# Small row vectors on another DMA queue, their transpose earlier, and one weight block in one load: a fused state-space and MLP kernel on one core

## The chip, the cores and the metric

The kernel runs on one core of a Trainium2 chip. The metric is the device time of one execution in microseconds (us). The profile is a recording of one such execution by the hardware profiler. Its span is a little shorter than the device time, because it begins with the first recorded instruction and ends with the last.

The engines are named as in the profile: PE is TensorE (matmuls and transposes), DVE is VectorE, ACT is ScalarE, POOL is GpSimd, and SP is SyncE, which here only issues transfers. SP, ACT and POOL each have a queue from which they can start DMA transfers.

## The reference, cut to what matters

A sequence `x` of 2048 rows and 640 columns goes through two branches, and a gate mixes them:

```python
g = sigmoid((x * gate_w).sum(-1, keepdims=True))
# A: a diagonal complex state-space layer
dt = exp(log_dt)
Lam_bar = exp(dt * Lam)                       # Lam = Lambda_re + 1j * Lambda_im, 640 values
B_bar = ((Lam_bar - 1.0) / Lam)[:, None] * B
Bu = x @ B_bar.T
for t in range(L): h = Lam_bar * h + Bu[t]    # the scan over the sequence
a = 2.0 * real(hseq @ C.T) + x * Dskip
# B: an MLP
b = gelu(x @ w1 + b1) @ w2 + b2               # w1: 640 x 1728, w2: 1728 x 640
return g * a + (1 - g) * b
```

Four small vectors are of interest here: `Lambda_re`, `Lambda_im` and `log_dt` with 640 values each, and `b1` with 1728.

## The kernel before: the parts that the change touches

The kernel is written as operations with an engine, an assumed duration, the tiles that they read and write, and a priority. A small list scheduler in the kernel's own source fixes each engine's order of instructions when the program is built: of the operations that are ready in its simulated time it takes the one with the lowest priority number. Only the order comes from it; on the chip the engines wait for each other by semaphores.

The transfers of the beginning, all on SP's queue, bring in `x` (first 512 rows) and `w1` in blocks of 128 rows:

```python
NW = 8; FW = NW * 128                         # the first pass covers 1024 of the 1728 columns of w1
WSPLIT = {1: 6, 3: 6}

def w1load(k, eng, prio):
    edges = [0] + ([WSPLIT[k] * 128] if k in WSPLIT else []) + [FW]
    for i, (f0, f1) in enumerate(zip(edges, edges[1:])):
        load(f"w1_{k}{i}", eng, f"l_w1{k}{i}", W1sb[:, k, f0:f1], B_w1[k * 128:(k + 1) * 128, f0:f1],
             [("w1", k, i)], prio=prio + 0.1 * i, lat=2.6)

load("xna", "sp", ...)                        # x, first two column blocks, rows as they are
w1load(0, "sp", 1); w1load(1, "sp", 1.3)
xtrans(0, range(KN, KN + 1), 1.6, 0.8)        # x, third column block, transposed by the DMA
w1load(2, "sp", 2)
xtrans(0, range(3, 4), 3, 0.8)
w1load(3, "sp", 4)
xtrans(0, range(4, 5), 4.5, 0.8)
w1load(4, "sp", 5)
# ... the rest of w1 (w1_r0, w1_r1), then B, transposed by the DMA in 512 and 128 rows
```

The small vectors are needed as columns, one value for each partition. They are loaded as rows of 128 values into one tile `rows`, which PE transposes in one instruction into bank 7 of PSUM; DVE copies the result to `cols`:

```python
ROWS = {"lre": (0, A_Lambda_re), "lim": (KP, A_Lambda_im), "ldt": (2 * KP, A_log_dt), "b1a": (3 * KP, B_b1[0:nmain])}
op("rz", "pool", 0.2, (), list(ROWS) + ["b1b"], f_rz, prio=-90)     # rows <- 0
for i, (nm, (r0, src)) in enumerate(ROWS.items()):
    src = src.rearrange("(k p) -> k p", p=128)
    load(nm, "pool", "l_" + nm, rows[r0:r0 + src.shape[0], :], src, [nm], prio=-50 + i, dur=1.0)
load("b1b", "act", "l_b1b", rows[RT:RT + 1, :]..., B_b1[nmain:F]..., ["b1b"], prio=-101, dur=1.2)

psC = PS[7][:, :].bitcast(BF16)[:, 0:128]
def f_cols():                                                       # line 446 of the profile
    return inc("pe", nc.tensor.transpose(psC, rows[:, :], ident[:, :]))
op("cols", "pe", 0.3, list(ROWS) + ["b1b", "ident"], [("bank", 7)], f_cols, prio=20.5)
def f_cols1():                                                      # line 451
    return inc("dve", nc.vector.tensor_copy(out=cols[:, :], in_=psC[:, 0:RT + 1]))
op("cols1", "dve", 0.2, [("bank", 7)], ["lcol", "b1col"], f_cols1, prio=-1000)
```

From `cols` a chain of short operations goes over ACT and DVE: `dt = exp(log_dt)`, `acol = dt * Lambda_re`, `thcol = dt * Lambda_im`, the angles reduced to one turn, their sines on ACT (lines 456 to 490). ACT loads a function table for exp, one for sin and one for GELU. Only then, in ACT's order, comes the first GELU, which has `b1` from `cols` as its bias.

PE's first pass over `w1` goes block by block of 128 rows (`k`), with one PSUM bank for each group of 128 columns (`jf`), so that it can begin with the first block and keeps all eight banks open until the last block. The first four matmuls are halves of 256 columns:

```python
def m1_first():
    seq = [(k, jf) for k in range(KD) for jf in range(NW)]          # KD = 5, NW = 8
    seq.remove((0, NW - 1)); seq.insert(seq.index((1, NW - 1)), (0, NW - 1))   # bank 7 begins late
    steps = [(0, 0, 0), (0, 1, 0), (0, 0, 1), (0, 1, 1)] + [(k, jf, None) for k, jf in seq if k or jf > 1]
    for k, jf, h in steps: ...                                      # one matmul each, line 640
    for jf in range(NW):                                            # GELU of each bank, line 649
        op(f"ge_0_{jf}", "act", ..., [("bank", jf), "b1col"], [("gl", 0, jf)], f_ge, prio=10)
```

After these 42 matmuls the second pass (line 662) takes the remaining columns of `w1`, beginning with bank 0, which the first GELU must have read by then. After it come the products with B (line 705), the scan on DVE, and so on for four quarters of the sequence; none of that is touched by the change.

Of the kernel before, what the change touches and what calls it, by code (L numbers as in the profile page):

```python
# [147 lines left out]
class Prog:  # L148
# [8 lines left out]
    def op(self, name, eng, dur, reads, writes, fn, prio=None, lat=0.0, after=()):  # L157
        deps = {}
        for k in reads:
            for w in self.last_w.get(k, ()):  # L160
                deps[w.idx] = w
        for k in writes:
            for w in self.last_w.get(k, ()):
                deps[w.idx] = w
            for r in self.last_r.get(k, ()):
                deps[r.idx] = r
        for a in after:
            deps[a.idx] = a
        deps = list(deps.values())
        E = self.E  # L170

        def run(eg, deps=deps, eng=eng, fn=fn):
            E.wait(eng, *[d.done for d in deps if not (eng == "pe" and d.eng == "pe")])
            return fn()

        it = self.sch.add(name, eng, dur, deps, run, prio=prio, lat=lat)
        for k in writes:
            self.last_w[k] = [it]
            self.last_r[k] = []
        for k in reads:  # L180
            self.last_r.setdefault(k, []).append(it)
        return it


def bass_gated_mix__ssm_conv_s5__dense_activation_gelu__prompt_kernel(
# [40 lines left out]
    with ExitStack() as es:  # L226

        def SB(name, shape, dt):
            return es.enter_context(nc.sbuf_tensor(name, list(shape), dt))
# [12 lines left out]
        rows = SB("rows", [128, 128], BF16)  # L242
        cols = SB("cols", [128, 3 * KP + NF], FP32)
# [10 lines left out]
        ident = SB("ident", [128, 128], BF16)  # L254
# [53 lines left out]
        op = pr.op  # L308
# [4 lines left out]
        def dma_inc(eng, ins, sem):  # L313
            SEM(sem)
            E.count.setdefault(sem, 0)
            ins.then_inc(sems[sem], 16)
            E.count[sem] += 16
            return (sem, E.count[sem])
# [11 lines left out]
        def load(name, eng, sem, dst, src, writes, prio, dur=0.5, lat=2.5, reads=(), after=()):  # L330
            def fn():
                with nc.allow_non_contiguous_dma(reason="columns of small vectors"):
                    return dma_inc(eng, engines[eng].dma_start(dst, src), sem)
            return op(name, eng, dur, reads, writes, fn, prio=prio, lat=lat, after=after)
# [19 lines left out]
            load_T(f"xT{q}_{ks[0]}", f"l_xT{q}_{ks[0]}", [(xT[q][:, ks[0]:ks[-1] + 1, :], x2[q * 512:(q + 1) * 512, ks[0] * 128:(ks[-1] + 1) * 128])],  # L354
                   [("xT", q, k) for k in ks], prio, dur)

        WSPLIT = {1: 6, 3: 6}

        def w1load(k, eng, prio):
            edges = [0] + ([WSPLIT[k] * 128] if k in WSPLIT else []) + [FW]  # L360
            for i, (f0, f1) in enumerate(zip(edges, edges[1:])):
                load(f"w1_{k}{i}", eng, f"l_w1{k}{i}", W1sb[:, k, f0:f1], B_w1[k * 128:(k + 1) * 128, f0:f1], [("w1", k, i)], prio=prio + 0.1 * i, lat=2.6)

        def w1tok(k, jf):
            return ("w1", k, int(jf >= WSPLIT.get(k, NW)))

# [15 lines left out]
        ROWS = {"lre": (0, A_Lambda_re), "lim": (KP, A_Lambda_im), "ldt": (2 * KP, A_log_dt), "b1a": (3 * KP, B_b1[0:nmain])}  # L382
# [5 lines left out]
        op("rz", "pool", 0.2, (), list(ROWS) + ["b1b"], f_rz, prio=-90)  # L388
        for i, (nm, (r0, src)) in enumerate(ROWS.items()):
            src = src.rearrange("(k p) -> k p", p=128)  # L390
            load(nm, "pool", "l_" + nm, rows[r0:r0 + src.shape[0], :], src, [nm], prio=-50 + i, dur=1.0)
        load("b1b", "act", "l_b1b", rows[RT:RT + 1, :].rearrange("o (a p) -> o a p", a=2),
             B_b1[nmain:F].rearrange("(o p) -> o p", o=1).unsqueeze(1).broadcast_to([1, 2, FL]), ["b1b"], prio=-101, dur=1.2)

# [25 lines left out]
        for i, (k, c0, c1) in enumerate(((0, 0, 2), (0, 2, 4), (1, 0, 2), (1, 2, 4))):  # L420
            bank = (7, 6, 5, 4)[i]
# [23 lines left out]
        def f_cols():  # L445
            return inc("pe", nc.tensor.transpose(psC, rows[:, :], ident[:, :]))

        op("cols", "pe", 0.3, list(ROWS) + ["b1b", "ident"], [("bank", 7)], f_cols, prio=20.5)

        def f_cols1():  # L450
            return inc("dve", nc.vector.tensor_copy(out=cols[:, :], in_=psC[:, 0:RT + 1]))
# [642 lines left out]
```

## Time and profile before

| | before |
|---|---|
| device time, median of 3 runs | 214.33 us (214.19 to 214.42) |
| span of the profile | 212.5 us |
| PE busy | 209.4 us, 99% |
| DVE busy | 190.0 us, 89% |
| ACT busy | 102.9 us, 48% |
| POOL busy | 6.4 us, 3% |
| granted PE clock | 1.0 |
| first matmul of the first pass (L640) | 4.58 us |
| row transpose on PE (L446) | 9.46 us |
| first GELU (L649) | 13.92 us |
| second pass (L662) begins | 14.75 us |

An L and a number is a line of the kernel's source. In a line of the chain the first number is the start in us, the second the duration, and `x21` the number of instructions merged in that piece. In a line of the timeline the form is the same, with the tile that is written and the tiles that are read (`out<-in`), and in square brackets the idle time before it with what ended it. `ACTq` and `SPq` are the queues' instructions that issue a transfer; the time shown is that of issuing it and not that of the transfer. What a transfer takes is given as the time from its issue to its landing.

### The profile page before, as it was taken

How to read it: one execution, taken by the hardware profiler on the slowest of the kernel's cores; microseconds unless marked ns; L12 is line 12 of the kernel's file. 1: busy time of each engine (PE TensorE's matmuls, PEld its weight loads, DVE VectorE, ACT ScalarE, POOL GpSimd, SP SyncE). 2: the span in 40 equal slices, each digit the busy share in tenths (PEclk: the TensorE clock that was granted, in tenths of full speed). 3: DMA queues.
4: the chain of work that ended last, by engine and by line, in shares of the span. 5: the costliest groups of instructions: out<-in, count | busy, mean ns of one | idle time of the engine just before them, and what ended most of it. 6: DMA issues, size and time to landing. Idle time of an engine off the chain costs nothing.

```text
span 212.5 us, 2752 instructions
## 1 busy us (share of the span) xinstructions
PE 209.4 (99%) x1102; PEld 104.8 (49%) x1102; DVE 190.0 (89%) x240; ACT 102.9 (48%) x177; POOL 6.4 (3%) x16
## 2 busy tenths in 40 slices
PE   8999999999999999999999999999999999999996
PEld 4444444444464444444464444444446444567775
DVE  2199999999999999999999999999999999497954
ACT  2099556667960253556671063455660027623330
POOL 5000000030000000000010000000010000000000
DMA  5999999999800020046375000002854000005711
GB/s 169 192 281 179 152 140 220 347 244 190 188 7 3 0 49 0 0 28 155 67 58 114 3 0 0 0 2 71 111 117 123 0 3 0 0 0 102 170 39 62
DMA packets 48879, 19.07 MB, mean 90 GB/s; under 512 B 41572, under 2 KB 47844, under 8 KB 48868
## 3 DMA queue, kind: packets, MB, share of 16 engines
q1 hardware_dynamic: 47136, 17.59, 40.2%
q0 software_dynamic: 1728, 1.32, 4.9%
q8 instruction: 8, 0.13, 0.3%
q14 instruction: 3, 0.02, 0.1%
q10 hardware_dynamic: 4, 0.00, 0.0%
HBM read 8.41 MB, written 2.63 MB: 52 GB/s over the span
## 4 chain that ended last, share of the span: by engine, by line
PE 96%; ACT 1%; DVE 1%; issue 0%
PE ps L662 22%; PE ps L705 20%; PE ps L929 20%; PE ps L978 15%; PE ps L792 7%; PE ps L841 5%; PE ps L640 2%; PE ps L415 1%; PE ps L683 1%; PE ps L940 1%; ACT L649 1%; PE ps L427 0%; ACT Gl L649 0%; PE ps L806 0%; DVE W1sb L875 0%
## 5 line engine op out<-in xcount | busy, mean ns | idle before, releaser
L662 PE MATMUL ps<-xT,W1sb 128*128 128x512 bf16 x220 | 48.1, 379 | 0.3 <-ACT Gl L649 0.3
L745 DVE TENSOR_TENSOR_SCAN W<-atab,V 128x1280 bf16<-128x1280 f32 x16 | 44.3, 2811 | 0.3
L705 PE MATMUL ps<-xT,BT 128*128 128x512 bf16 x200 | 43.8, 379 | 0.0
L929 PE MATMUL ps<-Gl,W2sb 128*128 128x512 bf16 (+1 forms) x234 | 42.7, 344 | 0.0
L669 ACT ACTIVATE Gl<-ps,cols 128x512 bf16<-128x512 f32 x44 | 29.9, 695 | 15.5 <-PE ps L662 15.5
L662 PEld LDWEIGHTS ps<-xT,W1sb 128*128 128x128 bf16 x220 | 21.4, 98 | 26.5 <-issue 0.8
L978 PE MATMUL ps<-Hb,CT 128*128 128x512 bf16 x150 | 32.9, 379 | 0.0
L929 PEld LDWEIGHTS ps<-Gl,W2sb 128*128 128x128 bf16 x234 | 22.9, 98 | 19.3
L705 PEld LDWEIGHTS ps<-xT,BT 128*128 128x128 bf16 x200 | 19.5, 98 | 23.7 <-ACT Gt L691 0.4
L714 ACT ACTIVATE U<-ps 128x512 bf16<-128x512 f32 x40 | 23.6, 600 | 14.4 <-PE ps L705 14.3
L947 ACT ACTIVATE E1T<-ps,cols 128x512 bf16<-128x512 f32 (+1 forms) x18 | 9.5, 624 | 36.0 <-PE ps L940 36.0
L978 PEld LDWEIGHTS ps<-Hb,CT 128*128 128x128 bf16 x150 | 14.4, 98 | 18.0 <-DVE W L496 0.3
L986 ACT ACTIVATE E2T<-ps 128x512 bf16<-128x512 f32 x15 | 9.1, 604 | 13.6 <-PE ps L978 13.6
L792 PE MATMUL ps<-W2sb,Gl 128*128 128x320 bf16 x104 | 14.8, 299 | 0.0
L615 DVE SCALAR_TENSOR_TENSOR trf<-xn,gwb 128x640 bf16<-128x640 bf16 x16 | 13.2, 823 | 0.4
L496 DVE TENSOR_TENSOR V<-V,W 128x1280 bf16<-128x1280 bf16 x16 | 12.5, 822 | 0.3
L496 DVE TENSOR_TENSOR Hb<-Hb,V 128x1280 bf16<-128x1280 bf16 x16 | 12.5, 821 | 0.3
L496 DVE TENSOR_TENSOR V<-mr,U 128x2560 bf16<-128x2560 bf16 x8 | 11.9, 1492 | 0.3
L792 PEld LDWEIGHTS ps<-W2sb,Gl 128*128 128x128 bf16 x104 | 10.1, 98 | 4.3 <-issue 0.3
L496 DVE TENSOR_TENSOR Hb<-c,W 128x2560 bf16<-128x2560 bf16 x8 | 11.9, 1490 | 0.2
L496 DVE TENSOR_TENSOR W<-mi,U 128x2560 bf16<-128x2560 bf16 x8 | 11.9, 1484 | 0.0
L496 DVE TENSOR_TENSOR V<-s,W 128x2560 bf16<-128x2560 bf16 x8 | 11.9, 1484 | 0.0
(95 smaller groups left out, 153.7 us busy)
## 6 DMA issues: line engine op xcount, KB each, us to landing
W2sb<-in_B_w_dram SPq DMA_DIRECT2D x1, 2080.0 KB, 8.6
out_dram<-xn SPq DMA_DIRECT2D x3, 640.0 KB, 4.8
xn<-in_A_x_dram POOLq DMA_DIRECT2D x2, 640.0 KB, 7.8
W1sb<-in_B_w_dram SPq DMA_DIRECT2D x3, 256.0 KB, 3.3
trf<-grow SPq DMA_DIRECT2D x3, 256.0 KB, 5.3
xn<-in_A_x_dram SPq DMA_DIRECT2D x1, 640.0 KB, 6.9
W1sb<-in_B_w_dram SPq DMA_DIRECT2D x1, 480.0 KB, 4.0
out_dram<-W1sb SPq DMA_DIRECT2D x3, 160.0 KB, 1.8
```

What stands on the lines that cost most here:

```text
L496: return inc("dve", nc.vector.tensor_tensor(out=o, in0=a, in1=b, op=o_))
L615: t = inc("dve", nc.vector.scalar_tensor_tensor(out=scr[:, :], in0=xn[q % 2][:, c, :], scalar=1.0, in1=gwb[:, :], op0=ALU.mult, op1=ALU.mu ...
L662: t = nc.tensor.matmul(PS[bank][:, :], W1sb[:, k, jf * 128:(jf + 1) * 128], xT[q][:, k, :], start=(k == 0), stop=(k == KD - 1))
L669: return inc("act", nc.scalar.activation(Gl[q % 2][:, jf, :], PS[bank][:, :], ACT.Gelu_apprx_tanh, bias=b1col[:, jf:jf + 1]))
L705: t = nc.tensor.matmul(PS[bank][:, :], BT[:, ci, kd, k * 128:(k + 1) * 128], xT[q][:, kd, :], start=(kd == 0), stop=(kd == KD - 1))
L714: return inc("act", nc.scalar.activation(dst, src, ACT.Copy, scale=1.0 if ci == 0 else -1.0))
L745: t = inc("dve", nc.vector.tensor_tensor_scan(out=g[:, ci, :], data0=a, data1=v[:, ci, :], initial=0.0, op0=ALU.mult, op1=ALU.add))
L792: t = nc.tensor.matmul(PS[bank][:, 0:HALF], Gl[q % 2][:, jf, t4 * 128:(t4 + 1) * 128], W2sb[:, jf, cols], start=False, stop=False, skip_gr ...
L841: t = nc.tensor.matmul(PS[bank][:, 0:n], H[b % NHB][:, ci, k, s * 128:(s + 1) * 128], CT[:, ci, k, cols], start=(i == 0), stop=(i == 2 * K ...
L929: t = nc.tensor.matmul(PS[bank][:, 0:t1 - t0], W2sb[:, jf, d * 128:(d + 1) * 128], Gl[q % 2][:, jf, t0:t1], start=(jf == 0), stop=False)
L947: return inc("act", nc.scalar.activation(E1T[:, d, t0:t1], PS[bank][:, 0:t1 - t0], ACT.Identity, bias=cols2[:, 0, d:d + 1]))
L978: t = nc.tensor.matmul(PS[bank][:, :].rearrange("p (s t) -> p s t", s=2), CT[:, ci, k, d * 128:(d + 1) * 128], Hb[:, 2 * (q % 2):2 * (q % ...
```

## The change

Three things are changed. The second block of 128 rows of `w1` is loaded in one transfer of 1024 columns and not in two of 768 and 256, which makes one transfer less for SP to issue. The four small vectors are loaded from ACT's queue, behind the one row that was loaded there already, and not from POOL's. And the row transpose on PE gets the priority 13.5 in place of 20.5; in the order of the built program it then stands behind 13 matmuls of the first pass and not behind 21, with three matmuls between it and the first one into bank 7 and not one. It is meant to have the vectors, and all that is computed from them, ready sooner. The input transposes of the state-space matrix B stay as they were, in 512 and 128 rows.

```diff
-        WSPLIT = {1: 6, 3: 6}
+        WSPLIT = {3: 6}
@@
         for i, (nm, (r0, src)) in enumerate(ROWS.items()):
             src = src.rearrange("(k p) -> k p", p=128)
-            load(nm, "pool", "l_" + nm, rows[r0:r0 + src.shape[0], :], src, [nm], prio=-50 + i, dur=1.0)
+            load(nm, "act", "l_" + nm, rows[r0:r0 + src.shape[0], :], src, [nm], prio=-100 + i, dur=0.4)
@@
-        op("cols", "pe", 0.3, list(ROWS) + ["b1b", "ident"], [("bank", 7)], f_cols, prio=20.5)
+        op("cols", "pe", 0.3, list(ROWS) + ["b1b", "ident"], [("bank", 7)], f_cols, prio=13.5)
```

## The prediction

> **What bounds the kernel now.** I read the busy shares first, then the chain that ended last in order of time, then the first 15 us engine by engine.
>
> From the page, the busy shares:
>
> ```profile
> PE 209.4 (99%) x1102; PEld 104.8 (49%) x1102; DVE 190.0 (89%) x240; ACT 102.9 (48%) x177; POOL 6.4 (3%) x16
> ```
>
> PE is the bound. The next view is the chain, piece by piece: start, duration, engine and line.
>
> ```profile
> 4.78 4.84 PE ps L640 x21
> 9.62 0.07 PE ps L446
> 9.69 0.02 issue
> 9.71 0.20 DVE cols L451
> ...
> 12.62 1.28 ACT L649
> 13.91 0.01 issue
> 13.92 0.70 ACT Gl L649
> 14.62 0.14 issue
> 14.75 5.56 PE ps L662 x25
> 20.31 10.79 PE ps L705 x50
> ```
>
> The reader is to see two things. From 14.75 us to the end the chain is matmuls back to back: 50 in 10.79 us is 0.216 us each, and nothing but removed matmuls or a removed wait could shorten that. Between 9.62 and 14.75 us, however, the chain leaves PE. It goes through the transpose of the row vectors (L446), their copy to `cols` (L451), the exp and sin work on DVE and ACT, a table load, and the first GELU. So PE waits there for the first GELU, which needs `cols`. PE alone, on its timeline in two narrow windows, gives the size of the two holes:
>
> ```profile
> 9.46 0.22 PE L446 MATMUL ps<-ident,rows 128*128 128x128 bf16 x1
> 9.51 0.84 PE L640 MATMUL ps<-xT,W1sb 128*128 128x512 bf16 x2
> ...
> 14.07 0.38 PE L640 MATMUL ps<-xT,W1sb 128*128 128x512 bf16 x1
> 14.75 0.59 PE L662 MATMUL ps<-xT,W1sb 128*128 128x512 bf16 x2 [0.30 <-ACT Gl L649]
> ```
>
> The page counts 0.30 us as idle, because matmuls are drawn with their pipeline. Start to start is the honest measure. From 14.07 to 14.75 is 0.68 us where 0.216 is due: **0.46 us lost**. Of the two matmuls at 9.51, the second starts at 9.96 (it takes 0.39 and the pair ends at 10.35): 0.45 where 0.216 is due, **0.23 us lost**. It is the first one into bank 7, which the transpose had used and DVE had not yet copied out. Together 0.70 us. Before 6 us PE is also slower (a 256-column matmul every 0.21 us), but that part does not hang on this change.
>
> [...]
>
> ```profile
> 0.97 1.18 ACTq L333 DMA_DIRECT2D rows<-in_B_b_dram  x1
> 1.26 1.60 SPq L333 DMA_DIRECT2D W1sb<-in_B_w_dram  x3
> 2.91 1.20 SPq L340 DMA_TRANSPOSE xT<-in_A_x_dram  x1
> ```
>
> ScalarE's one row load took 1.18 us to issue beside SyncE's loads, which took 0.53 each (1.60 / 3) for far more data. [...]
>
> **The change, part by part.**
>
> *W1's second block in one load.* Removed: one issue of SyncE, some 0.5 us (0.53 mean; the 64 KB one took 0.43). Before, the 192 KB part was issued at about 1.8 us and took 3.8 to land (5.6), the 64 KB part was issued at 2.44 and took 3.8 (6.2). The first matmul of this block is the tenth after the x transposes; the matmul that starts at 7.73 is the fourteenth, so the tenth starts four earlier, at 6.87. The whole block at about 6.2 is still 0.6 us ahead. All later SyncE loads could start up to 0.5 us earlier, but PE waits for none of them: the third block (issued at 4.16, 3.8 to land, 8.0) is needed by the seventeenth matmul, at 7.73 + 3 x 0.216 = 8.38 now; in the new order that is 0.05 for the transpose and 2 x 0.216 for two bank-7 matmuls later, 8.87. This part is worth about 0 by itself.
>
> *Transpose of the rows eight matmuls earlier.* In the changed program it stands behind 13 matmuls of the first pass instead of 21. The thirteenth starts at 7.51, so PE reaches the transpose at 7.73 instead of 9.46: 1.73 us earlier. Three matmuls now lie between it and the first one into bank 7 instead of one. Bank 7 was free 0.50 us after the transpose began (9.96 - 9.46), so now at 8.23; PE comes there at 7.73 + 0.05 + 3 x 0.216 = 8.43. That hole closes: -0.23.
>
> *The GELU chain.* From transpose to first GELU took 13.92 - 9.46 = 4.46 us, so the GELU could start at 12.19. Now it will wait for its own bank instead: bank 0's last matmul starts seven before the last of the pass, 14.07 - 7 x 0.216 - 0.23 = 12.33, and ends 0.38 later, 12.71. GELU 0.69 us plus the 0.14 of hand-over: bank 0 is free at 13.54. PE wants it at 14.07 - 0.23 + 0.216 = 14.06. That hole closes too: -0.46, with 0.5 us to spare. Later GELUs come every 0.6 us (four in 2.42) against PE's 1.08 per bank, so they only gain on PE.
>
> *The four row loads on ScalarE's queue.* This is where it can go wrong, since the transpose waits for all five row loads. On GpSimd the last was issued at 3.19 and landed 3.3 us later, at 6.5: 3 us before its use. On ScalarE they queue behind the 1.18 us load that ends at 2.15. If each takes SyncE's 0.53, the last is issued at 2.15 + 3 x 0.53 = 3.74 and, with the same 3.3, lands at 7.0, which is 0.7 before 7.73. ScalarE's first table load, now at about 4.3 instead of 2.18, ends near 5.6 (1.28 long), and its exp is wanted only at 8.2: free.
>
> Sum with the rows in time: -0.23 - 0.46 = -0.70, so 213.6 us. The rest of the program is the same work. The few exchanged places later (a gate tanh before instead of after a neighbour on ScalarE, the last state-space multiply on DVE ahead of an output sum) lie beside a PE that never waits, and the DVE chain, which starts from `cols`, begins 1.7 us earlier against 0.7 for PE, so its slack grows.
>
> **Rivals.**
>
> *The rows land late and PE waits at the transpose.* For it: 1.18 us for the only ScalarE issue we see; SyncE's 1.2 us transposes fall into the same stretch[...]. If all four take 1.18, the last is issued at 2.15 + 3 x 1.18 = 5.7, lands at 9.0, and PE stands 1.3 us: 213.6 + 1.3 = 214.9. Against it: the loads are tiny (5 to 13 rows of 256 B), and the long issue may be a cost of the first one only. Half-way (0.85 each) gives 4.7 + 3.3 = 8.0, a wait of 0.3: 213.9. Break-even is a landing at 8.4.
>
> *ScalarE's issues hold up SyncE's loads of W1 and x.* For it: [...] four more issues are put between SyncE's at 2.2 to 4.5 us. Against: SyncE's third load, beside ScalarE's, took at most some 0.15 longer than the 0.43 of the one behind it, and the saved 0.5 pays for most. The third block has 0.9 us of slack in the new order (8.0 against 8.87), so even a full half microsecond would cost nothing; a whole one would cost 0.1 to 0.3.
>
> *The gain turns up as a wait further on.* For instance at B's transposed load, which no issue change moves by more than 0.5 us. It is issued at 9.91 and takes 7.5 (17.4); PE wants it at 20.31 now, 19.6 then. X's second quarter, issued at 21.25, takes 6.1 (27.3) and is wanted at 31.1, then 30.4. Neither binds: time 213.6.
>
> **Range and chances.** The whole stake is 0.7 us of gain against some 1 to 2 us of possible new wait, under 1% of 214.33, so "within 2%" (4.3 us) is nearly sure. I give about one half to the rows in time (213.6), a quarter to a wait up to 0.7 (213.7 to 214.3), a quarter to more. That puts the middle at 213.85. Low end: the full gain and the spread of the runs of before (0.2 us), 213.4. High end: the four slow issues, 214.9 and a little, 215.1. Faster by over 2%: 0.005; within: 0.985; slower: 0.01.
>
> **What would show it.** Right: the row transpose at about 7.7 us; the second pass (L662) starting at about 14.05 with no idle time before it; the first GELU at about 12.7, released by PE and not by the table load; the last matmul about 0.7 us earlier. Wrong: PE idle at L446 behind a DMA of `rows`, with ScalarE's four issues spread over more than 3 us; or PE idle in L640 behind `W1sb`; or a first pass (L640) that starts later than 4.58.

## The result, and the profile after

| | before | after |
|---|---|---|
| device time, median | 214.28 us (213.52 to 214.42, 6 runs) | 213.09 us (212.42 to 213.41, 6 runs) |
| ratio after / before, 95% interval | | 0.9946 [0.9924, 0.9968] |
| span of the profile | 212.5 us | 211.3 us |
| first matmul of the first pass (L640) | 4.58 us | 4.88 us |
| row transpose on PE (L446) | 9.46 us | 7.26 us |
| first GELU (L649) | 13.92 us | 12.26 us |
| second pass (L662) begins | 14.75 us | 13.57 us |

The kernel became 1.19 us faster; the interval of the ratio, times 214.28, is 0.69 to 1.63 us. That is inside 2%, as predicted, but the median lies under the predicted range of 213.4 to 215.1: the gain was larger than the 0.70 us that the two holes could give.

The page of after, busy shares:

```profile
PE 208.1 (98%) x1102; PEld 104.4 (49%) x1102; DVE 190.1 (90%) x240; ACT 102.9 (49%) x177; POOL 4.2 (2%) x12
```

Then the chain that ended last in after, in order of time (start, duration, engine and line):

```profile
4.88 2.54 PE ps L640 x13
7.42 0.06 PE ps L446
7.48 6.26 PE ps L640 x29
13.74 5.40 PE ps L662 x25
19.13 10.79 PE ps L705 x50
```

Between 4.88 us and the end the chain never leaves PE. The whole detour of before, over `cols`, the exp and sin work, a table load and the first GELU, is gone. (The chain starts each piece where the one before it ended, so 13.74 here is the 13.57 of the timeline.) PE alone, on its timeline:

```profile
3.74 0.69 PE L427 MATMUL ps<-ident,xn 128*128 128x128 bf16 x8
4.88 2.54 PE L640 MATMUL ps<-xT,W1sb 128*128 128x256 bf16 x13 [0.45 <-DVE xT L433]
7.26 0.22 PE L446 MATMUL ps<-ident,rows 128*128 128x128 bf16 x1
7.31 6.42 PE L640 MATMUL ps<-xT,W1sb 128*128 128x512 bf16 x29
13.57 2.75 PE L662 MATMUL ps<-xT,W1sb 128*128 128x512 bf16 x12
```

The three pieces from 7.26 us on have no bracket: neither the bank-7 hole nor the GELU hole is left. One line says something else. The eight transposes of `x` (L427) took 0.69 us here and 1.03 in before: PE came to its full rate earlier in this execution, in the middle of these transposes. (PE began at half rate in both: in before 256 columns took 0.213 us in the first pass, in after 0.108, at full rate.) The prediction had put that aside, and it turns out to matter. Last, ACT's timeline of after:

```profile
0.97 1.19 ACTq L333 DMA_DIRECT2D rows<-in_B_b_dram  x1
2.20 0.31 ACTq L333 DMA_DIRECT2D rows<-in_A_Lambda_re_dram  x1
...
3.22 0.40 ACTq L333 DMA_DIRECT2D rows<-in_B_b_dram  x1
...
12.26 1.27 ACT L649 ACTIVATE Gl<-ps,cols 128x512 bf16<-128x512 f32 x2 [0.56 <-PE ps L640]
```

Only the first row load takes 1.19 us to issue; the next four take 0.31, 0.31, 0.32 and 0.40. And the first GELU now waits for PE, its own bank, and not for `cols` or a table.

One fact makes all profiles of this study comparable. From the start of the second pass to the start of the last matmul it is 195.57 us in every one of them (195.569 to 195.583), and the tail is 2.19 to 2.23. So a span is the start of the second pass plus 197.8 us, and within a span only what lies before that start has to be explained. (A device time is 1.3 to 2.0 us longer than its span; what the change does to that part is told below.) In the two profiles: the first pass begins 0.30 later in after (its first block of `w1` landed at 4.75 us and not at 4.40; the bracket at 4.88 names DVE, but DVE's first copy ended at 4.42, and in e1, e2 and e14 too the first matmul starts 0.135 us after this landing), and lasts 8.69 us and not 10.18. Of these 1.49 us the two holes are 0.70; 0.79 are still to be found.

### The profile page after: what moved, and what is told of

It is laid out like the page before. It is cut to its first block, busy times and chain, and to the rows that moved or that the text cites. A ratio compares the mean times of both kernels' runs of the same rounds, so it can differ in the third digit from the quotient of the medians.

```text
span 211.3 us, 2750 instructions
## 1 busy us (share of the span) xinstructions
PE 208.1 (98%) x1102; PEld 104.4 (49%) x1102; DVE 190.1 (90%) x240; ACT 102.9 (49%) x177; POOL 4.2 (2%) x12
## 3 DMA queue, kind: packets, MB, share of 16 engines
q0 software_dynamic: 1600, 1.32, 8.9%
## 4 chain that ended last, share of the span: by engine, by line
PE 98%; DVE 0%; issue 0%
PE ps L662 22%; PE ps L705 20%; PE ps L929 20%; PE ps L978 15%; PE ps L792 7%; PE ps L841 5%; PE ps L640 4%; PE ps L415 1%; PE ps L683 1%; PE ps L940 1%; DVE xT L433 0%; PE ps L806 0%; PE ps L427 0%; DVE W1sb L875 0%; PE ps L446 0%
## 5 line engine op out<-in xcount | busy, mean ns | idle before, releaser
L662 PE MATMUL ps<-xT,W1sb 128*128 128x512 bf16 x220 | 48.1, 379 | 0.0
L662 PEld LDWEIGHTS ps<-xT,W1sb 128*128 128x128 bf16 x220 | 21.5, 98 | 26.0
```

Source lines behind the costliest of these rows:

```text
L662: t = nc.tensor.matmul(PS[bank][:, :], W1sb[:, k, jf * 128:(jf + 1) * 128], xT[q][:, k, :], start=(k == 0), stop=(k == KD - 1))
```

## The experiments

Two theories stood against each other. **Two holes only** (theory H in the expectations): the change is worth 0.70, and the rest is the moment at which PE reaches full rate, which happened to be early in the runs of after. **A third wait** (theory L): the executions of before with an early full rate lose the advantage again, because PE then reaches the third block of `w1` before it has landed, and the change removes that wait as well.

### The parts, in their own place

**e1_after_again**: the changed kernel, as it is.

> The changed kernel once more, to see how its times spread and when PE's clock comes up. Theory H (only the two holes of the prediction, 0.23 and 0.46 us): the median settles near 213.6, and what was measured beyond it was luck with the clock. Theory L (the loads matter too: in executions where PE's clock comes up early, PE overtakes the loads of W1 in the kernel before but not in the changed one): the median stays near 213.1, 1.0 to 1.2 us below before, and the spread within the changed kernel (about 1 us) goes with the clock.

**e2_cols_only**: the row transpose early, the rows still on POOL's queue, `w1` still split. The assumed duration of 0.4 is only what the list scheduler needs for the early place; the loads are the same.

```diff
-load(nm, "pool", ..., prio=-50 + i, dur=1.0)
+load(nm, "pool", ..., prio=-50 + i, dur=0.4)
-op("cols", "pe", 0.3, ..., prio=20.5)
+op("cols", "pe", 0.3, ..., prio=13.5)
```

> Only the row transpose is moved to behind 13 matmuls; the rows stay on GpSimd's queue, W1's second block stays in two loads. Theory H: the whole gain, 213.6 (ratio 0.9967), with both holes closed. Theory L: 0.7 from the holes and some of the rest, since the move also puts two matmuls more ahead of the third block: 213.3 to 213.6. If the rows on GpSimd land after 7.3 us, PE waits at the transpose instead, and the gain is smaller in early-clock executions.

**e3_w1_only**: `w1`'s second block in one load, nothing else.

```diff
-WSPLIT = {1: 6, 3: 6}
+WSPLIT = {3: 6}
```

> Only W1's second block in one load; the rest as before, holes of 0.23 and 0.46 us included. Theory H: no difference, 214.3. Theory L: the third block lands about 0.45 us earlier, so executions with an early clock gain up to 0.4 us: median 214.0 to 214.2, lowest 213.0 to 213.4.

**e4_act_cols_split**: the changed kernel with `w1` split as before.

```diff
-WSPLIT = {3: 6}
+WSPLIT = {1: 6, 3: 6}
```

> The changed kernel with W1's second block still in two loads: rows on ScalarE's queue, transpose behind 13 matmuls. Theory H: the same as the changed kernel. Theory L: 0.1 to 0.4 us slower than the changed kernel of this call, because the third block lands about 0.45 us later.

Measured, with before at 213.75 us (213.12 to 214.30, 40 runs) on the same chip:

| | median (range, runs) | ratio to before, 95% | first pass begins, lasts; second begins (profile) |
|---|---|---|---|
| e1_after_again | 212.52 (212.22 to 213.16, 6) | 0.9953 [0.9935, 0.9971] | 4.44, 8.69; 13.13 |
| e2_cols_only | 213.25 (212.40 to 214.86, 22) | 0.9980 [0.9968, 0.9992] | 4.52, 8.70; 13.22 |
| e3_w1_only | 213.96 (213.00 to 215.97, 14) | 1.0028 [1.0005, 1.0051] | 4.56, 9.51; 14.07 |
| e4_act_cols_split | 213.02 (212.32 to 214.92, 11) | 0.9972 [0.9951, 0.9993] | 4.43, 9.47; 13.91 |

The gain of the changed kernel repeats: 1.23 us. Moving the transpose is needed for it, and `w1`'s load alone brings nothing here, although theory L expected up to 0.4 us in executions with an early full rate. (Of its three long runs, 215.50 to 215.97, no profile is kept; they stay unexplained.) But one profile does not speak for a median. Those of e1 and e2 are of their fastest runs (212.22 and 212.40 us): PE stood nowhere in either, and the first passes are equally short; yet e2's median is 0.73 worse. In e4 PE stood nowhere either, but its first pass lasted 0.78 longer. PE's timeline in e4:

```profile
4.43 3.32 PE L640 MATMUL ps<-xT,W1sb 128*128 128x256 bf16 x13
7.59 0.22 PE L446 MATMUL ps<-ident,rows 128*128 128x128 bf16 x1
```

The 13 matmuls before the transpose take 3.16 us from start to start, and 2.38 in after (4.88 to 7.26). The same work, with no wait, at another rate: half rate up to about 6.0 us, and full rate from then on. In before it came at about 6.1. Put side by side, the first passes of e4 and before last 9.47 and 10.18: 0.70 apart before rounding, which is the two holes and nothing else. And the 0.78 between e4 and after is what was still to be found: before had a late full rate in its profile, and after an early one. So a single profile of each kernel cannot be read without the moment of its full rate.

Not all of the gain is in the span. Every run's device time and span are on record, and here are their means on this chip:

| | queue of the rows | mean span | mean of device time less span (range) |
|---|---|---|---|
| before | POOL | 212.14 | 1.57 (1.32 to 1.92) |
| e1_after_again | ACT | 211.28 | 1.35 (1.32 to 1.39) |
| e2_cols_only | POOL | 211.63 | 1.65 (1.34 to 1.93) |
| e3_w1_only | POOL | 212.58; 212.10 without the three long runs | 1.62 (1.36 to 1.97) |
| e4_act_cols_split | ACT | 211.74 | 1.33 (1.27 to 1.38) |

e2 and e4 differ in the queue alone; PE, DVE and ACT have the same order of instructions in both. Their spans hardly differ, but outside the span e2 takes 0.3 us more, in the mean. So 0.2 to 0.3 us of what the change brings comes from taking the rows off POOL's queue, and lies where no profile shows it; what it is stays open. Inside the span the changed kernel gains 0.86, e2 0.51 and e4 0.40. The last two are less than the 0.70 of the two holes, and which wait of their unprofiled runs takes the rest stays open as well.

### The moment of full rate taken out

**e7_late_before** and **e8_late_after**: the warm-up matmuls go on longer, and the transposes of `x` wait for idle work on DVE, until 12.98 us. By then PE has long had its full rate, and the blocks of `w1` that mattered have landed. Nothing is left out; the idle work uses a tile that is written again later.

```diff
-for n in (512,) * 6 + (256,):
+for n in (512,) * 36:
+op("delay", "dve", 0.01, ["ident"], ["V", "delay"], f_delay, prio=-3000)   # 11 adds over 1280 columns
-op(f"xt{i}", "pe", ..., ["xna", "ident"], ...)
+op(f"xt{i}", "pe", ..., ["xna", "ident", "delay"], ...)
```

> The kernel before with PE's real work held back to about 12 us, so that the clock is full and all loads of the first pass have landed: only the holes are left. First pass about 9.4 us in every theory, the spread a few tenths of a us at most.

> The changed kernel held back in the same way: 0.70 us (0.65 to 0.75) faster than the held-back kernel before in both theories, first pass 8.69 us. If it is far from 0.70, the two holes are not what the change removes.

**e5_shift_before** and **e6_shift_after**: the loads and the `x` transposes all begin 4.9 us later, with the same order on every queue, and the warm-up lasts until then. So the loads stand to each other and to PE as in the real kernel, but PE has its full rate before the first pass, at 6.56 us in the profile of e5 and at 4.55 in that of e6.

```diff
-for n in (512,) * 6 + (256,):
+for n in (512,) * 18:
+tick("d_sp", 4, True, -9003); tick("d_act", 1, False, -9002); tick("d_pool", 2, False, -9001)   # idle DVE work
-load("xna", "sp", ...)
+load("xna", "sp", ..., reads=["d_sp"])          # the same for b1b with d_act and the POOL rows with d_pool
```

> The kernel before with everything but PE's warm-up shifted later by about 4 us (the first loads of all three queues wait for idle DVE work), so that PE's clock is always full when the first pass begins, with loads, transposes and waits in their old relation. Both theories: the spread of about 1.2 us shrinks to a few tenths, and the time is some 3 us longer. Theory H: PE shows the two holes of 0.23 and 0.46 us and no other wait, first pass about 9.4 us long. Theory L: a third hole of 0.3 to 0.6 us where PE waits for the third block of W1, first pass 9.7 to 10.0 us.

> The changed kernel with the same shift. First pass 8.69 us, as in the two profiles of the changed kernel whose clock was full from the start, and no hole. Theory H: 0.70 us faster than the shifted kernel before. Theory L: 1.0 to 1.3 us faster.

Measured, with before at 214.21 us (213.43 to 214.71, 9 runs):

| | median (range, runs) | ratio to before, 95% | first pass lasts |
|---|---|---|---|
| e7_late_before | 222.43 (222.20 to 222.76, 4) | 1.0385 [1.0360, 1.0409] | 9.41 |
| e8_late_after | 221.52 (221.42 to 221.54, 5) | 1.0341 [1.0319, 1.0363] | 8.71 |
| e5_shift_before | 218.62 (218.47 to 218.89, 4) | 1.0207 [1.0184, 1.0230] | 10.05 |
| e6_shift_after | 217.33 (217.24 to 217.43, 4) | 1.0145 [1.0123, 1.0168] | 8.71 |

The late pair gives the two holes alone: 9.41 − 8.71 = **0.70 us**. The spans agree, 220.8 in all four runs and 220.1 in all five. (The medians differ by 0.91; the other 0.2 is outside the spans, 1.66 us in the mean for e7 and 1.41 for e8.) That is the prediction's sum.

The shifted pair gives 1.29 us by the medians, 1.20 by the mean spans and 1.34 by the profiles; the profile of e5 is of its longest run (217.4, the other spans 217.1 to 217.2). PE's timeline of e5 (here L657 is the first pass and L463 the row transpose):

```profile
9.53 3.19 PE L657 MATMUL ps<-xT,W1sb 128*128 128x256 bf16 x16
13.22 1.24 PE L657 MATMUL ps<-xT,W1sb 128*128 128x512 bf16 x5 [0.50 <-DMA W1sb<-in_B_w_dram]
...
15.03 4.26 PE L657 MATMUL ps<-xT,W1sb 128*128 128x512 bf16 x19 [0.30 <-DVE cols L468]
19.58 1.67 PE L679 MATMUL ps<-xT,W1sb 128*128 128x512 bf16 x7 [0.29 <-ACT Gl L666]
```

And of e6:

```profile
9.47 2.56 PE L657 MATMUL ps<-xT,W1sb 128*128 128x256 bf16 x13
...
11.92 6.42 PE L657 MATMUL ps<-xT,W1sb 128*128 128x512 bf16 x28
18.18 3.19 PE L679 MATMUL ps<-xT,W1sb 128*128 128x512 bf16 x14
```

In e5 there are three brackets, in e6 none (`...` stands for the row transpose and one matmul between them). The first is the new one: the seventeenth matmul, the first of the third block, stood until the block's load had landed, at 13.08, and started 0.14 us after that. The sixteenth started at 12.34 us, so the step is 0.88 where 0.22 is due: **0.67 us**. The other two are the old ones, at bank 7 and at the GELU, 0.70 together by the late pair. The three make 1.37, against 1.34 between the two profiles. (The pieces hold 41 of the pass's 42 matmuls; the record of one is missing.)

### Is the third hole there in the ordinary kernel?

**e13_before_look1** to **e16_before_look4**: the kernel before, unchanged, one profile each.

> The unshifted kernel before, one more profile. If PE's clock is full before about 4.5 us: theory L says that PE waits 0.3 to 0.6 us for the third block of W1 at about 7.5 us, and the first pass takes 9.6 to 10.0 us; theory H says no such wait and a first pass of 9.4 us. If the clock is late (after 5.5 us), no third hole in either, and a first pass of about 10.1 us.

> As the look before: with an early clock a wait of 0.3 to 0.6 us for the third block by theory L, none by theory H; with a late clock none in either.

> As the look before: with an early clock a wait of 0.3 to 0.6 us for the third block by theory L, none by theory H; with a late clock none in either.

> As the look before: with an early clock a wait of 0.3 to 0.6 us for the third block by theory L, none by theory H; with a late clock none in either.

Single times: 213.33, 213.61, 213.87 and 213.84 us. PE's timeline in e15, which repeats the profile of before:

```profile
3.79 1.03 PE L427 MATMUL ps<-ident,xn 128*128 128x128 bf16 x8
4.61 4.96 PE L640 MATMUL ps<-xT,W1sb 128*128 128x256 bf16 x21
```

And in e14, whose transposes of `x` were at full rate:

```profile
3.70 0.67 PE L427 MATMUL ps<-ident,xn 128*128 128x128 bf16 x8
4.49 3.19 PE L640 MATMUL ps<-xT,W1sb 128*128 128x256 bf16 x16
8.07 1.24 PE L640 MATMUL ps<-xT,W1sb 128*128 128x512 bf16 x5 [0.40 <-DMA W1sb<-in_B_w_dram]
```

The chain of e14 at that place:

```profile
4.16 3.77 DMA W1sb<-in_B_w_dram
7.93 0.14 issue
8.07 1.24 PE ps L640 x5
```

So it is there. In e15 PE was slow until about 6.0 us, came to the third block late, and 21 matmuls follow each other without a bracket. In e14 it was early, and the third block, issued at 4.16 and landed at 7.93, stopped it. Step by step (start of the matmul before it to its start, less 0.216) the third hole is 0 in before and e15, 0.24 in e13, 0.56 in e14 and 0.57 in e16, whose block landed latest (8.17). The five spans lie between 211.95 and 212.54 us. An early full rate brings this kernel little, because the third block's landing is waiting behind it.

e3, with one load less ahead of the third block, came to full rate at the same moment as e16 (4.79 and 4.82 us). Its third block landed at 7.40, its first pass has no third hole, and it lasts 9.51 us and not 10.09. But e3's times show no gain (mean span 212.10 without the long runs, against 212.14), so how much the third hole costs an average execution isn't settled by these runs.

### Which part of the change closes it

The same shifted kernel, with parts of the change. **e9_shift_cols** has the edit of e2, **e10_shift_w1** that of e3, **e11_shift_act_cols** that of e4, and **e12_shift_pool_cols_w1** those of e2 and e3 together, so that of the whole change only the move to ACT's queue is missing. Each is the corresponding diff above on top of e5 (in e11 the rows need no wait of their own behind `b1b`).

> The shifted kernel before with only the row transpose behind 13 matmuls (rows on GpSimd, W1's second block in two loads). Theory L: the two old holes (0.70) are gone and the one before the third block shrinks from 0.67 to about 0.18, because the transpose and two bank-7 matmuls (0.05 + 0.43 us) now come ahead of it: first pass 8.7 to 9.0 us, time 217.4 to 217.7. Theory H: 217.9.

> The shifted kernel before with only W1's second block in one load. Theory L: the old holes stay (0.70), the third shrinks from 0.67 to 0.1 to 0.3, since the third block is issued some 0.46 us earlier: first pass 9.5 to 9.7 us, time 218.1 to 218.3. Theory H: no difference, 218.6.

> The shifted changed kernel with W1's second block in two loads again: transpose behind 13 matmuls, rows on ScalarE. Theory L: like the transpose alone on GpSimd rows (217.4 to 217.7, a hole of up to 0.3 before the third block); the queue of the rows makes no difference as long as they land before PE comes to them. If ScalarE's issues delayed SyncE's, the hole would be larger than in the GpSimd version.

> The shifted changed kernel with the rows back on GpSimd's queue. Theory L: no hole, first pass 8.7 us, time 217.3, equal to the shifted changed kernel within 0.15. If the rows land later from GpSimd than PE reaches the transpose (with a full clock, 2.4 us after the first pass begins), PE waits there, and the time is longer by that wait.

Measured, with before at 213.90 us (213.43 to 214.50, 7 runs). The spans of all four runs are given, since the rest of a span was the same on each of the chips used (197.8 us); e5 has 217.1 to 217.4 and e6 215.9 to 216.1:

| | median (range) | ratio to before, 95% | spans | first pass lasts |
|---|---|---|---|---|
| e9_shift_cols | 217.60 (217.51 to 217.99) | 1.0178 [1.0151, 1.0205] | 216.0 to 216.4 | 8.69 |
| e10_shift_w1 | 218.14 (218.07 to 219.66) | 1.0214 [1.0175, 1.0253] | 216.6, 216.6, 216.6, 218.3 | 11.08 |
| e11_shift_act_cols | 217.61 (217.30 to 218.07) | 1.0174 [1.0149, 1.0199] | 216.0 to 216.7 | 9.06 |
| e12_shift_pool_cols_w1 | 217.65 (217.60 to 217.78) | 1.0175 [1.0154, 1.0196] | 216.1 to 216.2 | 8.90 |

*The transpose alone* (e9) can do the whole of it: its profile has a first pass of 8.69, as short as e6. It puts one transpose (0.05) and two bank-7 matmuls (0.43) ahead of the third block, which moves the need for it by 0.48 us, from about 12.53 to 13.01; the block landed at 12.73. With the 0.14 us from landing to start that leaves a margin of 0.14, and the spans of its runs go up to 216.4.

*`w1` in one load alone* (e10) saves 0.5 to 0.8 us in the three runs at 216.6: SP issues the third block 0.48 us earlier (8.60 in place of 9.09), and it landed at 12.20 in place of 13.08, so that with PE at full rate it is in time. Its fourth run is another matter, told below. The gains of the two parts do not add up, since either closes the same hole.

*All but the queue* (e12), which theory L expected at 217.3, waits for the rows in its profile: the last one, from POOL, landed at 11.80, and in PE's timeline the transpose is late:

```profile
9.46 2.56 PE L657 MATMUL ps<-xT,W1sb 128*128 128x256 bf16 x13
12.05 0.22 PE L463 MATMUL ps<-ident,rows 128*128 128x128 bf16 x1
```

From the start of the thirteenth matmul it is 0.41 us to the transpose where 0.216 is due: 0.19 lost, and the first pass lasts 8.90 where e6 has 8.71. That POOL's queue is the reason isn't shown. The last row landed at 11.60, 11.19 and 11.70 in e5, e9 and e10 (POOL), and at 11.59 and 10.92 in e6 and e11 (ACT), so 11.80 may be scatter. *All but the one load* (e11) loses at another block than theory L expected, on PE's timeline:

```profile
16.74 1.89 PE L657 MATMUL ps<-xT,W1sb 128*128 128x512 bf16 x8 [0.21 <-DMA W1sb<-in_B_w_dram]
```

There the fifth block of `w1` landed at 16.60 (issued at 13.16), and PE, now without holes ahead of it, came there 0.37 us too early. In e6 it was issued at 12.74 and landed at 15.81: of the 0.80 us between the two, 0.42 are the issue and 0.37 the time to landing, which also varies (e9 and e5, issued as late as e11, landed at 16.27 and 16.18).

So the parts do different things. The transpose takes away the old holes. The one load gives the later blocks 0.42 to 0.48 us more margin, which shows once the holes are gone: e11's spans go up to 216.7 and average 0.3 us more than e6's. ACT's queue shows outside the span: device time less span averages 1.54 us in e12 and 1.50 in e9, and 1.35 in e11 and 1.33 in e6. Of e12's 0.3 us above e6 in the medians (on another chip) 0.1 is in the span and 0.2 outside.

## Why the prediction was wrong, and where it was right

**The two holes: right.** They are closed in every kernel with the early transpose, present in every one without it, and worth 0.70 us (late pair). Bank 0 was to be free 0.5 us before PE wants it; in after it starts at 12.26, with one GELU of 0.69 and 0.14 of hand-over the bank is free at 13.09, and PE wants it at 13.57: 0.48. The first GELU "released by PE and not by the table load" is what ACT's timeline shows.

**The time of the row transpose: right but for the rate.** "PE reaches the transpose at 7.73" counted 3.15 us from the start of the pass. e4, with the same late full rate, took 3.16; after took 2.38.

**The rows on ACT's queue: safer than feared.** The sum took 0.53 for each issue, and the rival 1.18. They took 0.31 to 0.40; the 1.18 belongs to the first load alone, and it stands at 1.17 to 1.19 in all 18 profiles. The last row was issued at 3.22 and not 3.74, and landed at 6.54 and not 7.0. With it falls the rival "the rows land late", to which half of the chances had gone in one size or another, and so the high end of 215.1. With an early full rate it is nearer than these numbers say: in e6 the last row landed 0.28 us before the transpose, and e12 shows 0.25 from that landing to the transpose.

**ACT holding up SP: did not happen.** The third block's issue took 0.64 us beside ACT's and 0.58 without, and started at 3.70 and not 4.16. It landed at 7.56 and not 7.99. The 0.06 us cost nothing; what they come from is not shown.

**A later wait: did not happen** in after, whose chain is on PE from 4.88 us to the end. e11 shows that one was near: the fifth block came 0.37 us too late there, by a later issue and a longer landing together. One of the prediction's signs of being wrong did come, a first pass that starts later than 4.58: it started at 4.88. That goes back to the landing of the first block of `w1` (4.75 us; in e1, the same program, 4.30, and the pass began at 4.44), and it made after slower by 0.30 us, so it isn't the cause of the miss.

**The step that failed** is this one of the part on `w1`: "All later SyncE loads could start up to 0.5 us earlier, but PE waits for none of them", with its "worth about 0 by itself", and the remark before it, that PE's slow rate before 6 us "does not hang on this change". The slack of 0.38 us behind it (8.38 − 8.0) was read from one execution, one with a late full rate, and 0.14 of it is the time from a landing to the start of the matmul (7.93 to 8.07 in e14). Where the full rate came earlier (e13, e14, e16), PE came to the third block before it had landed and stood 0.24 to 0.57 us; this wait was on the path in three of five profiles of before. The change closes it twice over, by the place of the transpose and by the earlier issue. The prediction had both numbers for it, 8.87 for the later need and 0.5 for the earlier issue, and counted them as slack alone.

A second step failed with it: "Sum with the rows in time: -0.23 - 0.46 = -0.70, so 213.6 us" takes PE's path for the whole device time, and the move to ACT's queue entered only as a risk of a late landing. It also shortens the time outside the span, by 0.2 us in the mean (1.57 in before, 1.35 in e1).

The sum in place of −0.70 is −0.70 less the mean third hole of the five profiles, (0 + 0.24 + 0.56 + 0 + 0.57) / 5 = 0.27, so −0.97 us inside the span, and some −0.2 outside: about −1.2, an estimate. Measured were −1.19 and, repeated, −1.23 in the medians. That the sum meets them so closely is luck: in the means of the repetition it is −0.86 inside the span and −1.07 in all, and the interval of 0.69 to 1.63 just holds 0.70 too. It is the profiles and the shifted pair, more than the ordinary times, that show the third hole.

**The low end** failed for the same reason. It allowed 0.2 us of spread, from three runs that happened to agree; 40 runs of before spread over 1.2 us. And the spread is not only noise added to a fixed gain: an early full rate, which before loses in part at the third block, is kept by after to the end, and the 0.6 us by which the time outside the span varies in before (1.32 to 1.92) is 0.1 in after (1.31 to 1.39).

The prediction took the rate from its one profile: 0.21 us for 256 columns before 6 us, 0.216 for 512 after that. It did not ask whether another execution has the same moment. In these traces full rate began between 3.45 us (e2) and about 6.1 us (before). What that moment costs in the first pass is small, 0.78 us between e4 and after, under 1% of the span. But the whole change was under 1% too, and the moment decides which wait PE meets.

## What to carry to other kernels

Before calling a transfer hidden, ask by how much and in which execution: a slack of 0.4 us read from one profile is no slack when the engine's own rate comes up at a moment that varied by 2.7 us here. Where a stage lies in the first microseconds, take several profiles of the same kernel, or delay the stage until the rate is settled, and list its waits again. Two edits that relieved the same wait did not add up here, but the second one can be the margin that makes the first one's gain steady (spans of 216.0 to 216.4 us in e9, 215.9 to 216.1 in e6). And take the span from the device time in every run: a change can act on the part that no profile shows, here by 0.2 to 0.3 us.

## What the runs showed of the hardware that was not expected

**The moment of full rate, and what records it.** The views give a granted clock of 1.0 from the start, also while PE makes half-rate steps (0.427 us for 512 columns, 0.107 for a transpose of 128). The trace has no clock record for that stretch. In 10 of the 18 traces the record begins with the moment of full rate itself, for instance at 3.92 us in after, 3.77 in e1 and 4.50 in e13, where the steps halve; in the other 8, before among them, there is none. Here the rate of the first microseconds had to be read from the steps.

**PE fell back to half rate in the middle of dense matmuls.** It did so in the profiled run of e10, at 219.66 us its longest. The table by stretches of one microsecond (length, busy time and number of instructions by engine, granted clock, DMA share, GB/s):

```profile
9.00:10.00 1.00, 0.89 (x11) 0.62 (x9) 0.88 (x4) 0.00 (x0) 0.00 (x0) 1.00 1.27 260
...
11.00:12.00 1.00, 1.00 (x4) 0.30 (x2) 0.00 (x0) 0.00 (x0) 0.00 (x0) 0.50 1.09 252
...
13.00:14.00 1.00, 1.00 (x5) 0.35 (x4) 0.00 (x0) 0.00 (x0) 0.00 (x0) 0.67 1.03 163
14.00:15.00 1.00, 1.00 (x7) 0.41 (x6) 0.00 (x0) 0.00 (x0) 0.00 (x0) 1.00 0.83 210
```

The granted clock is the third number from the right. It goes down to 0.50, with 4 matmuls touching that microsecond where 7 touch the one from 14 to 15 us. By the steps, PE was at half rate from about 10.3 us (a step of 0.235, then 0.427) to 13.7 us (0.407, then 0.216): 3.4 us. This fall the granted clock does show. PE's timeline of e10 shows what came before it:

```profile
0.78 5.36 PE L432 MATMUL ps<-const-bfloat16-1.0 128*128 128x512 bf16 x18 [0.78 <-PEq L1096]
8.68 0.62 PE L444 MATMUL ps<-ident,xn 128*128 128x128 bf16 x8 [2.54 <-DMA xn<-in_A_x_dram]
```

Its 18 warm-up matmuls took 5.36 us, less than in e9, e6 and e5 (5.84, 5.92, 6.89), so its full rate came earlier. PE then stood 2.54 us, and fell back 1.6 us after it had started again. The trace's clock record has the moments: full rate from 3.418, half rate from 10.245, full rate from 13.658. In e9, e6 and e5 PE stood 2.15, 2.04 and 1.11 us at the same place and did not fall back. So the fall came after the longest of the four gaps; that the gap caused it is a guess, and why the other three had no fall is not shown. This is one run, and the gap was put there by the experiment. For the long runs of e2, e3 and e4 (214.86 to 215.97) a granted clock of 1.0 is on record, against 0.992 in e10's. That speaks against such falls, but since the record can be missing, it doesn't exclude them.

**A small row load's issue.** On ACT's queue it took 0.31 to 0.40 us, and 1.17 to 1.19 for the first, which is also the one load there with a repeated source; no run tells the two reasons apart. On POOL's queue, in before, it took 0.52 to 0.68.

**Time outside the span that goes with the queue.** In the 36 runs of the six kernels with the rows on ACT's queue, the device time is 1.27 to 1.45 us longer than the span. In the 117 runs with the rows on POOL's queue for which both are on record it is 1.32 to 1.97 us, and 1.59 in the mean against 1.35.
